# Where the lower halves of an attention output wait for their sum: a head pair's own denominator buffer, or the next pair's place in the output tile

## The chip, the cores and the metric

The kernel runs on one core of a Trainium2 chip. Its time is the device time in microseconds (us) of one execution. The engines are TensorE (PE, with its weight loads listed as PEld), VectorE (DVE), ScalarE (ACT), GpSimd (POOL) and SyncE (SP, which here only issues DMA transfers). Each engine works through its own instructions in order and waits at the first one whose inputs or buffers are not ready.

## The reference

Causal attention with a multiplicative decay, for 8 batches x 8 heads, 576 positions, head size 64, followed by a feed-forward layer with a squared ReLU over the 4608 rows of 512:

```python
scores = q @ k.T / sqrt(64) + (cum[:, None] - cum[None, :])   # cum = cumsum(log(clip(f)))
scores = where(causal, -1e9, scores)
attn = exp(scores - max(scores)); attn = attn / (sum(attn) + 1e-9)
x = attn @ v                                                  # 64 heads -> (4608, 512)
out = relu(x @ w_in) ** 2 @ w_out                             # 512 -> 2048 -> 512
```

## The kernel before

The 64 heads run one after the other. A head has six units (`UNITS`): a block of up to 128 keys against a range of queries. One unit is one **slot**, so there are 384 slots, and a written schedule says for each slot what is traced in it: the score products of its unit (`score`), the products with v of the unit two slots back (`av_part`, `LAG = 2`), parts of `finish`, events of the heads to come, and a share of the feed-forward steps (`fill`, `mlp_half`). PE, ACT, DVE and POOL execute in the order of tracing. SP's transfers are ordered by the tile framework.

The feed-forward layer works in 18 chunks of 256 rows; a chunk has 16 steps of two halves, `mlp1` (12 products of 256 columns) and `mlp2` (6 products of 512 columns). A batch has 576 rows, 2.25 chunks, so the 48 slots of a batch get the halves of two chunks of the batch before (4 halves to 3 slots), in one batch of three (2 halves to a slot). `ready[b]` says from which slot on batch b's rows are to be used, two slots after `finish` part 3 of its last pair. What is left after the last slot is feed-forward work alone.

From head 14 on (`NWHOLE`), values are split into a rounded upper half and a rest, and the product of v with the probabilities has two halves in one PSUM bank: rows 0 to 63 and rows 64 to 127. There is one such bank (`banks["av"] = [0]` once the feed-forward layer runs). When the query range 256 to 575 of a head is complete (first slot of the next head), ACT copies the two halves out of the bank: the first (line 502) into the head's place in `xts`, the output tile of the batch (two buffers, `xt0` and `xt1`, in turns, a place of 576 columns for each pair of heads), the second (line 504) into `xl`. Only then may PE write queries 0 to 255 of the head into the bank (line 464, one slot later); these are copied out in the same way.

`finish` runs once for each pair of heads, in four parts, at `(h + 1) * 6 - 1` plus the four numbers of `DIVIDE`, h being the odd head:

- part 0 loads the partial sums of the probabilities that `store_sums` (line 454) wrote to DRAM (line 526)
- part 1: DVE adds `xl` to x (line 535), reduces the sums and takes the reciprocals (537, 540), and two DMAs store them to DRAM (542)
- part 2 loads them again, spread over the partitions, into a tile named `den` (549)
- part 3: POOL multiplies x by `den` (551)

`xl` and part 2's tile share the name `den`, which has one buffer. Thus the `xl` of a pair can only be written when the multiplication of the pair before has read its reciprocals. With `(2, 4, 5, 6)`, and counting slots from the first slot of the even head that follows the pair, the parts lie in slots 1, 3, 4 and 5, and the next pair's first `xl` copy in slot 6.

Around it, in the slots of each head: POOL's selects of the causal mask (401), POOL's subtractions for the next head's lower halves (311 in slot 1, 314 in slot 3), DVE's rounding of q and k (303, 304 in slot 0), the row maxima of the next head (336 on PE, 342 on DVE; slots 1.5 to 4), which SP stores into the row that the next head's first score product reads (347), the cumulative row of the head after (257), and the split of finished x for the feed-forward layer (`split_x`, 568 and 569), which at the end of a batch is traced in the slot of part 3.

Of the kernel before, what the change touches and what calls it, by code (L numbers as in the profile page):

```python
# [9 lines left out]
F32 = mybir.dt.float32  # L10
# [26 lines left out]
def decay_attention_relu2_kernel(  # L37
# [20 lines left out]
    NH, D, _, S = qk.shape  # L58
    P = 2 * D
    H = 8  # L60
# [4 lines left out]
    NCC = DM // P  # L65
# [10 lines left out]
    NWHOLE = 14  # L76
    DEPTH = 4
    cpool = ctx.enter_context(tc.tile_pool(name="cpool", bufs=1))
    wk = ctx.enter_context(tc.tile_pool(name="wk", bufs=2))
# [5 lines left out]
    def bank(use):  # L85

        turn = banks[use] or banks["s"]
        b = turn.pop(0)
        turn.append(b)
        return psum.tile([P, 512], F32, name=f"bank{b}")  # L90
# [153 lines left out]
    NU = len(UNITS)  # L244
    state = {}
    xts = {}
# [27 lines left out]
    def replicated(h):  # L274

        return h // 2 == H // 2 - 1
# [179 lines left out]
    def av_split(st, acc, u, o, i, first, last):  # L456

        j = UNITS[u][0]
        ph, pl = st["p"][u]
        vhl = st["vhl"][:, j]  # L460
        high = acc[:, o], vhl, ph[:, i]
        low = acc[:D, o], vhl[:, :D], pl[:, i]
        for k, args in enumerate((high, low) if first else (low, high)):
            nc.tensor.matmul(*args, start=first and k == 0, stop=last and k == 1)  # L464

    def av_part(h, u, low):

        j, q0, q1 = UNITS[u]
        s0, s1 = (q0, min(q1, QA)) if low else (max(q0, QA), q1)
        if s0 >= s1:  # L470
            return
        st = state[h]
        first = u == (NU - 1 if low else 0)
        last = u == NU - 2
        if first:
            st["av"] = bank("av")
        acc = st["av"]
        base = 0 if low else QA
        o, i = slice(s0 - base, s1 - base), slice(s0 - q0, s1 - q0)
        if h < NWHOLE:  # L480

            vr = st["vr"].rearrange("p j d -> p (j d)")
            d = st["vr"].shape[2]
            vr = vr[:, j * d:min(j * d + P, NJ * d)]
            nc.tensor.matmul(acc[:vr.shape[1], o], vr, st["p"][u][:, i], start=first, stop=last)
        else:
            av_split(st, acc, u, o, i, first, last)
        if last:
            n = QA if low else S - QA
            if not low:  # L490
                if h % H == 0:
                    xts[h // H] = wk.tile([P, NCC, S], F32, name=f"xt{h // H % 2}", bufs=1)
                if replicated(h):

                    st["den"] = state[h - 1]["den"] if h % 2 else wk.tile(
                        [P, 2 * DM], F32, name=f"w{2 * NF - 3}", bufs=1,
                    )[:, :S]
                if h >= NWHOLE:
                    st["xl"] = state[h - 1]["xl"] if h % 2 else wk.tile([P, S], F32, name="den", bufs=1)
            o = (h % 2) * D  # L500
            x = xts[h // H][o:o + D, (h % H) // 2, base:base + n]
            nc.scalar.copy(out=x, in_=acc[:D, :n])
            if h >= NWHOLE:
                nc.scalar.copy(out=st["xl"][o:o + D, base:base + n], in_=acc[D:, :n])  # L504
            elif replicated(h):
                nc.scalar.copy(out=st["den"][o:o + D, base:base + n], in_=acc[D:, :n])
            else:
                nc.scalar.copy(out=qkraw[D:D + 1, h % 2, base:base + n], in_=acc[D:D + 1, :n])
# [142 lines left out]
    NA = H * NU  # L651


    DIVIDE = (2, 6, 9, 13), (2, 4, 5, 6)
    DIRECT = {1: 3, 3: 4}
    MAXIMA = (-3, -2.5, -2, -1.5, -1, -0.5), (1.5, 2, 2.5, 3, 3.5, 4)
    SPLIT = 0, 1, 1, 3
# [9 lines left out]

    def fin(h, part):

        return (h + 1) * NU - 1 + (DIRECT if replicated(h) else DIVIDE[h >= H])[part]  # L670

    avs = {}
    for n, (h, u) in enumerate(slots):
# [2 lines left out]
    for h in range(1, NH, 2):  # L676
        for part in DIRECT if replicated(h) else range(4):
            fins.setdefault(fin(h, part), []).append((h, part))
    last_slot = max(fins)
    ready = [fin(b * H + H - 1, 3) + 2 for b in range(B)]  # L680

    def fill(n, part):
# [79 lines left out]
    for n in range(-2 * NU, last_slot + 1):  # L762
        if n == 0:
            opening = len(tc.nc.cur_bb.bb.instructions)
        live = 0 <= n < len(slots)
        split_last()
        if live:
            h, u = slots[n]
            score(h, u)
            if h >= NWHOLE:  # L770
                unsplit.append((h, u))
        for ha, ua in avs.get(n, ()):
            if ua < NU - 1:
                av_part(ha, ua, False)
            else:
                av_part(ha, ua, True)
                av_part(ha, ua - 1, True)
        for args in fins.get(n, ()):
            finish(*args)
        for do in events.get((n, 0), ()):  # L780
            do()
        wr = RATES[0 if n < -9 else 1 if n < -6 else 2 if n < -3 else 3 if n < 0 else 4 if n < ready[0] else 5]
        cv(wr / 2)
        fill(n, 0.5)
        for do in events.get((n, 1), ()):
            do()
        cv(wr / 2)
        fill(n, 1.0)
# [45 lines left out]
```

## Time and profile before

| | |
|---|---|
| median of 3 runs | 1341.64 us (1337.22 to 1342.75) |
| the profiled execution's own time | 1340.81 us |
| its span, first to last instruction | 1338.8 us |
| PE busy / DVE / ACT / POOL | 1197.0 / 798.7 / 780.3 / 411.7 us |
| mean granted PE clock | 0.964 of full speed |

The span is 2.0 us shorter than the execution's own time. Up to about 228 us the first 14 heads and the preparation of the weights run, from there to about 1180 us the 50 heads with split values, then feed-forward work alone. An engine's busy time is an average over these stages; the idle time that stands in brackets in a timeline, with what ended it, tells where an engine waited.

### The profile page before, as it was taken

The page shows a single profiled execution, that of the slowest core. Times are in us where ns is not written, and L with a number is a line of the kernel's source. Part 1 is how long each engine was busy: PE and PEld are TensorE (multiplying, and loading weights), DVE is VectorE, ACT ScalarE, POOL GpSimd, SP SyncE. Part 2 cuts the span into 40 slices and gives each one's busy share as a digit, 9 for nine tenths or more (in the row PEclk, how much of TensorE's full clock was granted, in tenths as well). Part 3 has the DMA queues.
Part 4 walks back from the last instruction along what each step waited for, and adds up shares of the span by engine and source line. Part 5 has one row for each costly group of instructions (what it writes and reads, how often), then busy time and mean ns, then how long its engine had stood idle before and what let it go on. Part 6 is the DMA issues. An engine that isn't in the chain of part 4 may idle for free. (4 is left out here: it accounts for less than half of the span.)

```text
span 1338.8 us, 22723 instructions
## 1 busy us (share of the span) xinstructions
PE 1197.0 (89%) x7302; PEld 1053.6 (79%) x7302; DVE 798.7 (60%) x2132; ACT 780.3 (58%) x2008; POOL 411.7 (31%) x668
## 2 busy tenths in 40 slices
PE   4877999898888888999999888889988898989998
PEld 3556878787777777889899777778887787879997
DVE  7657665676666666666666666666666666631211
ACT  3655666566655665666666556656666556643443
POOL 4545452333333333322322233333332333200000
PEclk9989999999998999999999999999999999999999
DMA  7877612111211112111121111112111211000000
GB/s 190 185 160 171 165 35 53 39 41 30 55 38 43 37 39 54 30 41 38 41 55 19 50 33 46 39 39 50 30 46 39 54 34 46 20 26 1 17 16 16
DMA packets 124073, 72.36 MB, mean 54 GB/s; under 512 B 106008, under 2 KB 106008, under 8 KB 123956
## 3 DMA queue, kind: packets, MB, share of 16 engines
q1 hardware_dynamic: 122836, 66.80, 20.8%
q0 software_dynamic: 1120, 4.13, 1.6%
q8 instruction: 58, 0.95, 0.3%
q14 instruction: 59, 0.48, 0.1%
HBM read 60.36 MB, written 10.34 MB: 53 GB/s over the span
## 5 line engine op out<-in xcount | busy, mean ns | idle before, releaser
L604 PE MATMUL bank<-w,gh 128*128 128x512 f32 x1152 | 418.9, 405 | 0.0
L581 PE MATMUL bank<-xh,w 128*128 128x256 f32 x2304 | 346.8, 294 | 8.8 <-DVE xh L568 4.1
L581 PEld LDWEIGHTS bank<-xh,w 128*128 128x128 f32 x2304 | 312.2, 196 | 16.8 <-issue 4.9
L604 PEld LDWEIGHTS bank<-w,gh 128*128 128x128 f32 x1152 | 224.9, 195 | 40.8 <-ACT gh L591 0.3
L592 DVE TENSOR_TENSOR gl<-g,gh 128x256 fp32r<-128x256 f32 x288 | 122.6, 426 | 207.3 <-ACT gh L591 206.6
L604 PE MATMUL bank<-w,gl 128*128 128x512 f32 x576 | 232.3, 403 | 3.1 <-DVE gl L592 3.0
L589 ACT ACTIVATE r<-bank 128x256 f32<-128x256 f32 x288 | 110.1, 382 | 159.8 <-PE bank L581 146.4
L401 POOL TENSOR_SCALAR_AFFINE_SELECT p<-p 128x128 f32<-128x128 f32 x200 | 65.5, 327 | 415.5 <-ACT p L399 307.3
L581 PE MATMUL bank<-xl,w 128*128 128x256 f32 x1152 | 192.4, 291 | 0.0
L415 DVE TENSOR_TENSOR pl<-p,ph 128x320 fp32r<-128x320 f32 x200 | 133.8, 669 | 75.9 <-ACT ph L414 75.5
L464 PE MATMUL bank<-ph,vhl 128*128 128x320 f32 (+4 forms) x350 | 109.2, 312 | 71.2 <-ACT den L504 70.8
L581 PEld LDWEIGHTS bank<-xl,w 128*128 128x128 f32 x1152 | 166.0, 200 | 0.0
L342 DVE CUSTOM_DVE_ANT_0 bank<-bank,mz 128x256 f32<-128x256 f32 (+4 forms) x320 | 133.9, 433 | 22.3 <-PE bank L336 17.8
L464 PEld LDWEIGHTS bank<-ph,vhl 128*128 128x128 f32 x350 | 67.8, 194 | 86.4 <-ACT den L504 82.3
L415 DVE TENSOR_TENSOR pl<-wmag,ph 128x320 fp32r<-128x320 f32 x100 | 45.9, 459 | 146.3 <-ACT ph L414 146.3
L414 ACT CAST ph<-p 128x320 fp32r<-128x320 f32 x200 | 81.2, 406 | 87.8 <-POOL p L401 87.2
L336 PE MATMUL bank<-rk 66*128 66x320 f32 (+9 forms) x384 | 111.0, 318 | 18.9 <-DMA rk<-qkraw 10.7
L590 ACT ACTIVATE g<-r 128x256 f32<-128x256 f32 x288 | 120.5, 418 | 11.6 <-DVE gl L592 2.5
L604 PEld LDWEIGHTS bank<-w,gl 128*128 128x128 f32 x576 | 112.6, 195 | 17.7 <-DVE gl L592 4.0
L591 ACT ACTIVATE gh<-r 128x256 fp32r<-128x256 f32 x288 | 115.7, 402 | 0.0
L381 PE MATMUL bank<-rk 67*128 67x320 f32 (+4 forms) x300 | 90.0, 300 | 13.6 <-DMA rk<-tcol 12.3
L399 ACT ACTIVATE p<-bank 128x320 f32<-128x320 f32 x200 | 75.5, 378 | 37.5 <-PE bank L384 36.2
(94 smaller groups left out, 1791.2 us busy)
## 6 DMA issues: line engine op xcount, KB each, us to landing
qkraw<-in_qk SPq DMA_DIRECT2D x50, 288.0 KB
out<-osb SPq DMA_DIRECT2D x36, 256.0 KB
v<-in_v SPq DMA_DIRECT2D x56, 160.0 KB
den<-rdr SPq DMA_DIRECT2D x62, 144.0 KB
w<-in_w_in SPq DMA_DIRECT2D x16, 512.0 KB
w<-in_w_out SPq DMA_DIRECT2D x16, 512.0 KB
rk<-in_qk POOLq DMA_DIRECT2D x14, 288.0 KB, 5.3
rl<-in_qk SPq DMA_DIRECT2D x14, 288.0 KB
```

The source lines that it names most:

```text
L336: nc.tensor.matmul(ps[:m, :n], st["r2"][:rows, q0:q0 + m], st["kl0"][:rows, k0:k0 + n], start=True, stop=True,)
L342: nc.vector.tensor_tensor_reduce(out=ps[:m, :n], in0=ps[:m, :n], in1=mz[:m, mo:mo + n], op0=ALU.add, op1=ALU.min, scale=-1.0, scalar=init, ...
L381: nc.tensor.matmul(ps[:kn, :n], st["kl0"][:D + 3, k0:k0 + kn], st["r2"][:D + 3, q0:q1], start=True, stop=False,)
L414: nc.scalar.copy(out=ph[:, :n], in_=p[:, :n])
L415: nc.vector.tensor_tensor(out=pl[:, :n], in0=p[:, :n], in1=ph[:, :n].bitcast(F32), op=ALU.subtract,)
L464: nc.tensor.matmul(*args, start=first and k == 0, stop=last and k == 1)
L581: nc.tensor.matmul(ph[:, :T], w[:, s, cc], x[:, cc, :], start=(cc == 0 and k == 0), stop=(cc == NCC - 1 and k == 2),)
L589: nc.scalar.activation(out=r, in_=ph[:, :T], func=AF.Relu)
L590: nc.scalar.activation(out=g, in_=r, func=AF.Square)
L591: nc.scalar.activation(out=gh, in_=r, func=AF.Square)
L592: nc.vector.tensor_tensor(out=gl, in0=g, in1=gh.bitcast(F32), op=ALU.subtract)
L604: nc.tensor.matmul(po, g[:, ts], w[:, s], start=(fc == 0 and k == 0), stop=(fc == NF - 1 and k == 2),)
```

## The change

For heads 14 and up, `xl` no longer is a tile `den`. It is the next pair's place in the output tile (`pair = h // 2 + 1`; for the last pair of a batch that is the first place of the next batch's tile, which is therefore allocated one pair earlier; for the last pair of all a further tile). The parts of `finish` get a third row of `DIVIDE` for these heads, and the second row (now only heads 8 to 13) changes too:

```diff
-                if h % H == 0:
-                    xts[h // H] = wk.tile([P, NCC, S], F32, name=f"xt{h // H % 2}", bufs=1)
+                pair = h // 2 + 1
+                for b in (h // H, pair // NCC if h >= NWHOLE else 0):
+                    if b not in xts:
+                        xts[b] = wk.tile([P, NCC, S], F32, name=f"xt{b % 2}", bufs=1)
...
                 if h >= NWHOLE:
-                    st["xl"] = state[h - 1]["xl"] if h % 2 else wk.tile([P, S], F32, name="den", bufs=1)
+                    st["xl"] = xts[pair // NCC][:, pair % NCC, :]
...
-    DIVIDE = (2, 6, 9, 13), (2, 4, 5, 6)
+    DIVIDE = (2, 6, 9, 13), (2, 4, 6, 7), (3, 5, 6, 8)
...
-        return (h + 1) * NU - 1 + (DIRECT if replicated(h) else DIVIDE[h >= H])[part]
+        return (h + 1) * NU - 1 + (DIRECT if replicated(h) else DIVIDE[(h >= H) + (h >= NWHOLE)])[part]
```

Counted as above, the parts lie in slots 2, 4, 5 and 7 for heads 14 and up. `ready[b]` moves two slots with part 3 for batches 1 to 7.

## Rows read from the trace of the kernel before

**Rows 1.** the page: busy us of each engine over the whole span

```profile
PE 1197.0 (89%) x7302; PEld 1053.6 (79%) x7302; DVE 798.7 (60%) x2132; ACT 780.3 (58%) x2008; POOL 411.7 (31%) x668
```

**Rows 2.** PE's waits from 230 to 1180 us: total us, times, longest

```profile
PE bank L464 <- ACT den L504: 69.7, 40, 3.9
PE bank L381 <- DMA rk<-tcol: 12.3, 25, 0.9
```

**Rows 3.** waits of all engines over the span: total us, times, longest

```profile
POOL xt L551 <- DMA den<-rdr: 99.2, 31, 17.3
...
ACT den L504 <- POOL xt L551: 54.5, 24, 3.7
...
DVE xh L568 <- POOL xt L551: 40.1, 7, 6.7
```

**Rows 4.** PE's timeline: start us, us, what, in brackets the wait before it

```profile
266.80 0.58 PE L464 MATMUL bank<-ph,vhl 128*128 128x256 f32 x1 [3.43 <-ACT den L504]
...
1106.60 0.31 PE L381 MATMUL bank<-rk 67*128 67x320 f32 x1
...
1111.04 0.25 PE L381 MATMUL bank<-rk 67*128 67x192 f32 x1
...
1121.48 0.39 PE L381 MATMUL bank<-rk 67*128 67x320 f32 x1 [0.47 <-DMA rk<-tcol]
...
1123.54 0.31 PE L381 MATMUL bank<-rk 67*128 67x320 f32 x1
...
1127.06 0.58 PE L464 MATMUL bank<-ph,vhl 128*128 128x256 f32 x1 [3.05 <-ACT den L504]
...
1132.04 0.25 PE L381 MATMUL bank<-rk 67*128 67x192 f32 x1
...
1163.05 0.38 PE L464 MATMUL bank<-ph,vhl 128*128 128x256 f32 x1 [1.75 <-ACT den L504]
```

**Rows 5.** POOL's timeline around the same two heads

```profile
1109.20 0.29 POOL L401 TENSOR_SCALAR_AFFINE_SELECT p<-p 128x128 f32<-128x128 f32 x1 [4.39 <-ACT p L399]
1109.46 1.42 POOL L311 TENSOR_TENSOR rl<-qkraw,rk 64x576 fp32r<-64x576 f32 x1
1112.47 0.29 POOL L401 TENSOR_SCALAR_AFFINE_SELECT p<-p 128x128 f32<-128x128 f32 x1 [1.59 <-DVE tcol L342]
...
1125.16 1.40 POOL L551 TENSOR_TENSOR xt<-xt,den 128x576 f32<-128x576 f32 x1 [3.41 <-DMA den<-rdr]
```

**Rows 6.** stretches: length, busy us of engines, granted PE clock, DMA share, GB/s

```profile
1127.06:1145.55 18.49, 17.47 (x104) 15.86 (x104) 13.26 (x34) 12.17 (x33) 5.74 (x9) 0.91 0.17 49
...
655.00:740.00 85.00, 85.00 (x565) 77.94 (x564) 53.36 (x143) 56.51 (x146) 24.41 (x39) 1.00 0.16 38
...
266.00:573.00 307.00, 270.51 (x1665) 242.96 (x1665) 199.74 (x551) 187.96 (x491) 100.96 (x153) 0.94 0.17 41
...
763.00:1180.00 417.00, 370.21 (x2302) 332.52 (x2302) 270.67 (x743) 257.16 (x674) 136.10 (x208) 0.95 0.17 39
```

**Rows 7.** SP's timeline: transfers issued around the long wait

```profile
1117.78 1.15 SPq L542 DMA_DIRECT2D rdr<-sums  x2
1119.03 1.79 SPq L347 DMA_DIRECT2D rk<-tcol  x3
1121.24 1.14 SPq L549 DMA_DIRECT2D den<-rdr  x2
1122.48 0.39 SPq L257 DMA_DIRECT2D rk<-cum_dr  x1
```

**Rows 8.** timeline of POOL and DVE in the batch with three chunks

```profile
613.21 1.43 POOL L551 TENSOR_TENSOR xt<-xt,den 128x576 f32<-128x576 f32 x1 [0.85 <-DMA den<-rdr]
613.29 1.50 DVE L428 TENSOR_TENSOR wmag<-wmag,p 128x128 f32<-128x128 f32 x1
```

**Rows 9.** DVE's timeline: the last read of an output tile's part

```profile
1135.59 0.96 DVE L569 TENSOR_TENSOR xl<-xt,xh 128x768 fp32r<-128x768 f32 x1
```

**Rows 10.** PE's timeline where the attention has ended

```profile
1195.51 2.04 PE L581 MATMUL bank<-xh,w 128*128 128x256 f32 x8 [4.14 <-DVE xh L568]
```

## The prediction

> **What bounds the kernel now.** I read the page first. PE is busy for 1197.0 us of 1338.8 [rows 1], no other engine for more than 60% of it, so PE sets the time and what matters is where PE stands still or runs slowly. PE's own waits in the 50 split heads come next: one line holds nearly everything, 69.7 us in 40 waits of line 464 for ACT's copy out of the single accumulator bank [rows 2]. A second line, 12.3 us in 25, waits for the row maxima. The list of all waits then shows what stood behind that copy: ACT's `xl` copy waited 54.5 us in 24 cases for POOL's multiplication, and that one waited for the transfer of the reciprocals, 99.2 us in 31 [rows 3]. So the chain is: reciprocals land, POOL multiplies, `den` comes free, ACT copies `xl`, PE may write the bank.
>
> PE's timeline splits the 40 waits. Twenty are long, from 3.43 us (the first, at 266.80) to 1.75 us (the last, at 1163.05) [rows 4]; added up they are 59.1 us, 2.95 each. They belong to the even heads, whose `xl` is the first into `den`. The other twenty are 69.7 - 59.1 = 10.6 us, 0.53 each: the odd heads, whose `xl` goes into a tile already free, and who wait just for the two copies. The batch with three chunks (about 573 to 763 us) has none: with two halves in every slot its slots are long enough, and PE is busy for 85.00 of 85.00 us [rows 6].
>
> The waits cost twice. In 655 to 740 us the granted clock is 1.00; in the head that begins with the wait at 1127.06 it is 0.91 over 18.49 us [rows 6]: after such a wait PE has stretches at the lower level, 1.2 instead of 2.4 GHz. Over the two-chunk stretches it is 0.94 (307 us) and 0.95 (417 us).
>
> **The change part by part.**
>
> *The long waits.* The next pair's place is written by nobody before slot 6 of the following head pair and was last used a batch earlier, so the even head's copies find it free, like the odd head's now. 20 x (2.95 - 0.53) = 48.4 us go. Bounds: nothing gained if another condition holds the copy (below), 59.1 if even the ordinary wait is covered. I take 48.4.
>
> *The clock.* Lost time is 0.06 x 307 + 0.05 x 417 = 39 us [rows 6]; by the one head, 0.09 x 18.49 = 1.7 us each, it is 20 x 1.7 = 33. Heads with only the short wait return to the full level, so I expect the loss to go with the long waits, and take 36. Bounds: 0 (the clock falls anyway) and 39. A check by the slots: with the long wait it is 8.50 us from the score product at 1123.54 to that at 1132.04, without it 4.44 (1106.60 to 1111.04) [rows 4]. The difference, 4.06, is 2.5 of wait and 1.5 of clock, and 20 x 4.06 = 81, against my 48.4 + 36 = 84.4, in which the batch ends weigh more.
>
> *SP's order.* Part 1 moves from slot 3 to slot 4, and its two reciprocal stores with it. SP issues the stores at 1117.78 for 1.15 us, and only then three transfers of row maxima, 1.79 us [rows 7]. The first of these three (slot 3) is the one that the next head's score product needs; it came 0.47 us late at 1121.48 [rows 4]. Two of the three should now go ahead of the stores. Of the 12.3 us most belong to heads with these stores: bounds 0 and 12.3, I take 8 gained.
>
> *When the reciprocals land now.* The stores move back by two transfers (2/3 of 1.79, 1.2 us), and so do the loads: `den` was there at 1125.16 [rows 5], now about 1126.3. Slot 7 begins at 1123.54 less the 0.47, at 1123.1. In a head without a long wait POOL's select of that slot starts 2.6 us after the score product (1106.60 to 1109.20) and takes 0.29 [rows 4, 5], so POOL reaches the multiplication at 1126.0 and waits 0.3 us instead of 3.41. Behind it are the 1.40 us of the multiplication, then 1.42 of the subtraction in line 311, to 1129.1; the next select is due 5.9 us after the score product (1106.60 to 1112.47), at 1129.0. That just fits. What has no cover left is small: if `den` lands later, selects, ACT's and DVE's roundings and, two slots on, PE's products with v are late by as much.
>
> *DVE beside POOL.* Today the multiplication falls into the stall. In slot 7 DVE is at work. In the three-chunk batch, where POOL multiplies at 613.21 for 1.43 us, a DVE addition of 128 columns that starts at 613.29 ends only with it, after 1.50 us [rows 8]. So DVE can lose between 0 and 1.4 us for each pair. Whether PE feels it: bounds 0 and 24 x 1.4 = 34 us. There PE had no wait, but its slots are long. I take 0.2 us each, 5 us. The Trainium skill ("SBUF — State Buffer", section "Who interferes with whom") says that a DVE instruction with two SBUF inputs and a GpSimd one that reads SBUF share a read interface, and that the later one stands until the other is done. The trace agrees with its 1.50 us. By that rule alone each pair pays a whole multiplication and the sum below would be 1254.4 - 5 + 34 = 1283; by my value it is 1254.4. It speaks against this change, and is a rival below.
>
> *The cumulative row.* SP issues it right behind the loads of `den` (1122.48) [rows 7]; they come about 1.2 us later now, while the maxima that read the row lose the cover of the long wait. Bounds 0 to 0.5 us in each pair; I take 3 us in all.
>
> *Ends of batches.* `split_x` stays in the slot of part 3, so DVE still waits there for POOL (40.1 us in 7 [rows 3]). With `den` landing about when it is asked for, 5.7 us become some 2. PE's share in this is already in the long waits; I count nothing more. The output tile's earlier allocation needs the buffer's last reader gone: the read that began at 1135.59 ended at 1136.55 [rows 9], and the copies that would now write there are those before PE's resumption at 1163.05 [rows 4], 26 us later; two slots take some 5 us of that. No cost.
>
> *The tail.* After the last slot PE waits 4.14 us for the last split [rows 10]. Part 1 comes one slot later, and the feed-forward halves are stretched by two slots, so the chain is longer by one slot of pure feed-forward work and covered by two: at 4/3 halves to a slot of some 1.4 us each, 1.9 us gained. I take 2.
>
> *Heads 8 to 13* get one slot more before part 2: POOL's wait there delays little on PE. Nothing counted, 2 us either way.
>
> The sum, against the profiled execution's 1340.8 us: 1340.8 - 48.4 - 36 - 8 - 2 + 5 + 3 = **1254.4 us**. The median of the runs shown is 0.8 us above that execution, so 1255.
>
> **The rivals.**
>
> *A new wait in slots 7 to 9.* POOL's multiplication and line 311 back to back hold DVE's operands or the selects, and PE stands for about 1 us in each of 24 pairs: 24 us more than the sum, 1278, or 1288 where some of these also cost clock. For it: the 1.50 us addition [rows 8] and a fit with no reserve on POOL. Against: PE's products use results two slots old, and a slot with two halves gives 4.4 us. The rule of the "SBUF" page in the Trainium skill is this rival's mechanism. Chance 0.11.
>
> *The clock falls all the same.* The waits go, but the two short waits in slots 6 and 7 are enough to lower it once for each pair: 1254 + 36 = 1290. Against: the odd heads have the short wait too, and keep the clock. Chance 0.06.
>
> *The change doesn't do what it says.* ACT's copy waits for something else of the output tile, an earlier reader of the buffer or the addition of part 1, which reads the place that the next pair's x is copied to. Then about 1340. Against: the addition is traced two slots ahead of that copy, and the buffer is free 26 us ahead. Chance 0.04.
>
> *Slower.* One mechanism: the reciprocals land so late that POOL, standing at the multiplication in slot 7, holds the selects behind it and with them PE. In the old place POOL's wait cost 4.1 us for a pair. POOL would be through with line 311 at 1129.1, and PE can bear about 2 us more; so it decides when `den` lands some 6 us later than I work out, and at 7 us all 24 pairs pay 1 us more than before: 1365. Nothing on SP's queue between stores and loads takes so long. Chance 0.03.
>
> **How the numbers follow.** My forecast has 0.76. The time is its own, 1255. Its own spread: all gains and no cost, with 39 for the clock and 12 for the row maxima, is 1340.8 - 48.4 - 39 - 12 - 2 = 1239; with DVE's and the row's costs at half their bounds, about 1268. The range goes up to the first rival's 1288 and leaves out the last three: 1240 to 1288. Under 0.5% (6.7 us) a change of this kernel can't be told from none. Faster by more: 0.76 + 0.11 + 0.06 = 0.93; within: 0.04; slower: 0.03.
>
> **What would show it.** Right: no wait of ACT for POOL's multiplication, PE's waits at the v products all about 0.5 us, 25 to 30 us in all; granted clock 0.99 or 1.00 between 266 and 1100 us; two-chunk batches shorter by about 16 us and the three-chunk one nearly unchanged; two row-maxima transfers ahead of the reciprocal stores on SP. Wrong: POOL still waits over 2 us for `den`; DVE's rounding in slots 7 and 8 above 1.5 us with PE waiting for it; a clock below 0.97 without long waits.

## The result and the profile after

The changed kernel takes 1234.4 us (median of 4 runs, 1231.83 to 1238.2), the kernel before, run beside it, 1339.4 us (4 runs, 1336.16 to 1342.75). The ratio is 0.9218, with a 95% interval from 0.918 to 0.9256: faster by 105 us where 86 were forecast, and 5.6 us below the lower end of the range. The profiled execution took 1231.83 us, with a span of 1230.0. The lines of the kernel after stand 4 lower from about line 492 on: 502 is now 506, 504 is 508, 542 is 546, 549 is 553, 551 is 555, 568 is 572, 581 is 585, 589 is 593, 592 is 596, 604 is 608.

The page of the changed kernel: busy us of each engine, as in [rows 1].

```profile
PE 1158.4 (94%) x7302; PEld 1020.7 (83%) x7302; DVE 820.5 (67%) x2132; ACT 787.3 (64%) x2008; POOL 409.3 (33%) x668
```

PE has the same 7302 instructions and is busy for 38.6 us less: the same products at a mean granted clock of 0.994 instead of 0.964. DVE has the same 2132 instructions and is busy for 21.8 us *more*; to that we come back.

PE's waits in the split heads of the changed kernel: total us, times, longest, as in [rows 2].

```profile
PE bank L336 <- DVE rk L304: 17.2, 38, 0.8
PE bank L381 <- DVE tcol L342: 5.3, 5, 3.2
PE bank L464 <- ACT xt L508: 1.8, 2, 1.2
...
PE bank L381 <- DMA rk<-tcol: 1.0, 2, 0.5
```

The waits for ACT's copy out of the bank were 69.7 us in 40. The twenty long ones are gone, as forecast; but the twenty short ones, which were to stay, are gone too, but for 1.8 us in 2. The row maxima's transfers are late for 1.0 us instead of 12.3. Two waits are new, and the forecast's sum has neither: 17.2 us in 38 (1.5 in 2 before), at the products for the row maxima (line 336), for DVE's rounding of q and k; and 5.3 us in 5, at the score products (line 381), for DVE's row maxima (line 342). The five stand in heads 17, 25, 33, 49 and 57, right behind the ends of batches.

Waits of POOL and DVE over the whole span after, as in [rows 3].

```profile
POOL xt L555 <- DMA den<-rdr: 27.6, 7, 17.2
...
DVE xh L572 <- POOL xt L555: 14.1, 7, 3.4
```

The wait in the middle of [rows 3], ACT's for POOL's multiplication, has no counterpart any more. POOL's waits for the reciprocals fall from 99.2 us in 31 to 27.6 in 7; one of some 17 us, at the last multiplication of all, is in both.

Three stretches of the changed kernel (two chunks, three chunks, two chunks), columns as in [rows 6].

```profile
266.00:527.00 261.00, 252.83 (x1657) 229.51 (x1656) 202.90 (x542) 189.16 (x486) 101.33 (x150) 0.99 0.21 48
527.00:700.00 173.00, 171.19 (x1123) 155.42 (x1122) 117.33 (x297) 114.52 (x296) 49.32 (x79) 1.00 0.16 40
700.00:1054.00 354.00, 340.99 (x2237) 307.62 (x2236) 280.40 (x740) 253.56 (x654) 136.01 (x203) 1.00 0.20 47
```

The granted clock is 0.99 to 1.00 where it was 0.94 and 0.95.

Where the 109 us between the two spans went follows from three marks on PE's timeline, head 14's first score product, head 63's first, and the end:

| stretch | before | after | difference |
|---|---|---|---|
| up to head 14 | 208.5 | 204.4 | -4.1 |
| heads 14 to 62 | 950.4 | 850.0 | -100.4 |
| rest | 180.0 | 175.5 | -4.5 |

In the middle stretch PE is busy for 859.65 us before and 821.36 after (clock 0.96 and 1.00), and idle for 90.8 and 28.7. The 38.3 us of busy time are not clock alone: of the feed-forward products of 256 columns the stretch holds 24 fewer after, the two halves that now come behind the start of head 63. At 1.10 us for eight (line 585 at 307.86, shown below) they are some 3 us. So about 35 us of the 100 are clock, 3 are work that moved, and 62 are waits.

### The profile page after: what moved, and what is told of

Read it like the earlier page. It is cut to its first block, busy times and chain, and to the rows that moved or that the text cites. A ratio compares the mean times of both kernels' runs of the same rounds, so it can differ in the third digit from the quotient of the medians.

```text
span 1230.0 us, 22744 instructions
## 1 busy us (share of the span) xinstructions
PE 1158.4 (94%) x7302; PEld 1020.7 (83%) x7302; DVE 820.5 (67%) x2132; ACT 787.3 (64%) x2008; POOL 409.3 (33%) x668
## 4 chain that ended last, share of the span: by engine, by line
PE 42%; DVE 6%; ACT 5%; issue 2%; DMA 1%; POOL 0%; SPq 0%; POOLq 0%; DVEq 0%; ACTq 0%
PE bank L585 18%; PE bank L608 17%; PE bank L464 3%; PE bank L336 2%; PE bank L384 1%; PE bank L381 1%; DVE wmag L428 1%; ACT ph L414 1%; DVE pl L415 1%; DVE bank L342 1%; DMA den<-rdr 1%; DVE gl L596 1%; ACT g L594 1%; ACT xt L508 1%; ACT r L593 1%
## 5 line engine op out<-in xcount | busy, mean ns | idle before, releaser
L585 PE MATMUL bank<-xh,w 128*128 128x256 f32 x2304 | 330.3, 286 | 4.2 <-DVE tcol L342 2.2
L585 PEld LDWEIGHTS bank<-xh,w 128*128 128x128 f32 x2304 | 302.3, 190 | 11.5 <-DVE tcol L342 2.3
L608 PEld LDWEIGHTS bank<-w,gh 128*128 128x128 f32 x1152 | 217.6, 189 | 38.8 <-ACT gh L595 0.3
L585 PE MATMUL bank<-xl,w 128*128 128x256 f32 x1152 | 185.2, 283 | 0.0
L415 DVE TENSOR_TENSOR pl<-p,ph 128x320 fp32r<-128x320 f32 x200 | 119.4, 597 | 63.4 <-ACT ph L414 60.4
L585 PEld LDWEIGHTS bank<-xl,w 128*128 128x128 f32 x1152 | 158.4, 190 | 0.0
L336 PE MATMUL bank<-rk 66*128 66x320 f32 (+9 forms) x384 | 118.7, 324 | 34.8 <-DVE rk L304 17.2
L428 DVE TENSOR_TENSOR wmag<-wmag,p 128x320 f32<-128x320 f32 (+3 forms) x250 | 127.2, 509 | 1.7
L336 PEld LDWEIGHTS bank<-rk 66*128 66x128 f32 (+3 forms) x384 | 70.0, 185 | 48.3 <-DVE rk L304 22.6
L464 PE MATMUL bank<-ph,vhl 128*128 128x320 f32 (+4 forms) x350 | 103.1, 295 | 2.4 <-ACT xt L508 2.4
```

The costliest lines, as they stand in the source:

```text
L336: nc.tensor.matmul(ps[:m, :n], st["r2"][:rows, q0:q0 + m], st["kl0"][:rows, k0:k0 + n], start=True, stop=True,)
L415: nc.vector.tensor_tensor(out=pl[:, :n], in0=p[:, :n], in1=ph[:, :n].bitcast(F32), op=ALU.subtract,)
L428: nc.vector.tensor_tensor(out=total[:, q0:q1], in0=total[:, q0:q1], in1=p, op=ALU.add,)
L585: nc.tensor.matmul(ph[:, :T], w[:, s, cc], x[:, cc, :], start=(cc == 0 and k == 0), stop=(cc == NCC - 1 and k == 2),)
L608: nc.tensor.matmul(po, g[:, ts], w[:, s], start=(fc == 0 and k == 0), stop=(fc == NF - 1 and k == 2),)
```

## The experiments

Two things stood against each other as causes. The change moves `xl` to another buffer, and it moves the parts of `finish`; with part 3, though, `ready[b]` moves by two slots, and the feed-forward halves are paced from `ready[b]`. At 4 halves to 3 slots the slots of a head that get two halves are numbers 1 and 4 before, and 0 and 3 after (counted from 0 within a head). I call this the *phase* of the halves. The phase can be set by itself with a constant in `fill`:

```diff
-        r0 = ready[b - 1]
-        r1 = ready[b] if b < B else r0 + H * NU
+        r0 = ready[b - 1] + PACE * (b > 1)
+        r1 = ready[b] + PACE if b < B else r0 + H * NU
```

**The buffer alone (e1_buffer_only).** The changed kernel with the old slots:

```diff
-    DIVIDE = (2, 6, 9, 13), (2, 4, 6, 7), (3, 5, 6, 8)
+    DIVIDE = (2, 6, 9, 13), (2, 4, 5, 6), (2, 4, 5, 6)
```

> The kernel before with xl in the next pair's place and nothing else; all numbers of DIVIDE as before, so the feed-forward halves stand in the same slots. Phase theory (the part of the gain that I missed comes from the two slots by which ready moves: the slot in which ACT copies the bank then holds two halves instead of one, and hides the copies): the long waits go, the short ones of about 0.5 us stay in all 40 heads, the row maxima still come late; 1250 to 1262 us, some 20 us of PE waiting for the copies. Slots theory (the later parts themselves brought it, by SP's order and POOL's freedom): also 1250 to 1262. If the buffer is worth all of it: 1233.

Measured: 1295.2 us, ratio 0.9679 (0.9637 to 0.972). That is 33 us above the upper end of what I expected: the later parts are worth far more than I took. PE's largest waits from 226 to 1150 us:

```profile
PE bank L464 <- ACT xt L508: 17.2, 34, 1.0
PE bank L464 <- DVE pl L415: 17.2, 5, 4.7
PE bank L381 <- DMA rk<-tcol: 14.4, 25, 1.3
```

The first line is the step of the forecast by itself: the copies' long waits are gone, the short ones stay, 0.5 us each. The second is new, and with it most of what is lost lies at the ends of the batches: against the same kernel with the later parts and the same slots for the feed-forward halves (e2 below), heads 14 to 62 take 23.5 us longer, and 19 of these fall on the five pairs of heads behind such an end. PE, POOL and DVE there, each from its own timeline of this kernel:

```profile
553.82 0.58 PE L464 MATMUL bank<-pl,vhl 128*64 128x256 f32 x2 [2.81 <-DVE pl L415]
...
554.41 2.02 PE L585 MATMUL bank<-xh,w 128*128 128x256 f32 x8
```

```profile
551.18 1.40 POOL L555 TENSOR_TENSOR xt<-xt,den 128x576 f32<-128x576 f32 x1 [3.15 <-DMA den<-rdr]
```

```profile
552.61 0.36 DVE L572 CAST xh<-xt 128x256 fp32r<-128x256 f32 x1 [5.78 <-POOL xt L555]
```

Read them from POOL on: `split_x` is queued on DVE in the slot of part 3 and stands 5.78 us for POOL, which stands for the reciprocals. Behind it on DVE is the remainder `pl` (line 415, at 553.35) that PE's v product needs; PE waits 2.81 us, and the eight products of line 585 that follow take 2.02 us (granted clock 0.50, the lower level, from 553.80 to 557.00) instead of the 1.10 that they take at the full level (at 307.86 below). In the kernel before, DVE stood there as long, but most of it lay inside PE's long wait for the bank, and little was seen as PE's own, from 230 to 1180 us:

```profile
PE bank L464 <- DVE pl L415: 3.5, 5, 1.0
```

DVE's waits at this place are 39.6 us in 7, as before the change; with the later parts they are 14.1.

**The phase, four ways.** The changed kernel with the phase of before (PACE = 1) and with the third one there is (PACE = 2), the kernel before with the phase of after (PACE = 2), and the buffer alone with the phase of after (the first experiment with PACE = 2):

> The changed kernel with the pacing of the halves one slot later still, three slots after the kernel before, which puts the two-halves slots where they were (4 halves to 3 slots repeat every 3 slots). Phase theory: the short waits come back in 40 heads, 1245 to 1260 us, the row maxima stay in time. Slots theory: no change, 1230 to 1238, since parts and buffer are those of the changed kernel.

> The kernel before with the pacing alone two slots later; xl still in den. Phase theory: a second half of 1.4 us stands in front of each wait for the copies, so the short waits vanish and the long ones shrink from 2.95 to about 1.5 us, some without a fall of the clock: 1270 to 1310. A rival by which the pacing does it all and the buffer nothing: 1235. Slots theory: 1335 to 1342.

> The first of these kernels (xl moved, DIVIDE as before) with the pacing two slots later, as ready sets it in the changed kernel. Phase theory: buffer and pacing are the whole change, 1230 to 1240. Slots theory: like the first, 1250 to 1262, with row maxima still late by about 0.5 us in half of the heads.

> The changed kernel with the pacing two slots later still: the third of the three places that the slots with two halves can have (slots 2 and 5 of a head). Phase theory: the slot of the copies has one half again and so has the next one, the short waits return in 40 heads with 0.5 to 1 us: 1250 to 1275. If only the number of slots mattered and not where the halves stand: 1230 to 1238.

Median us, with the interval of the ratio to the kernel before that ran beside each (1334.8 us for the first four of these kernels, 1341.4 for the third phase):

| | old phase | new phase | third phase |
|---|---|---|---|
| old buffer, old slots | 1339 (before) | 1319.8 (0.9823 to 0.9912) | |
| new buffer, old slots | 1295.2 (0.9637 to 0.972) | 1272.0 (0.9484 to 0.9548) | |
| new buffer, new slots | 1269.9 (0.9466 to 0.9531) | 1234.4 (0.918 to 0.9256) | 1316.2 (0.9767 to 0.9848) |

All directions were expected and most sizes missed: the old phase costs 35 us where I had expected 11 to 26, the third one 82 where I had expected 16 to 41, and the two kernels with the new phase and old slots stay above their ranges by 10 and 32. By the ratios, times 1339.4 us and good to some 5 us, all three parts have a share that none of the others replaces: the buffer 43 and 47 us, the slots 24 and 40, the phase 18, 22 and 37, each more where the others are there already. The old buffer with the new slots was not run.

Why the phase matters is seen where PE asks for the bank. PE's timeline of the changed kernel with the old phase, from the slot in which ACT copies:

```profile
481.86 0.31 PE L381 MATMUL bank<-rk 67*128 67x320 f32 x1
...
482.45 0.40 PE L608 MATMUL bank<-w,gh 128*128 128x512 f32 x1
...
483.85 0.31 PE L381 MATMUL bank<-rk 67*128 67x320 f32 x1
...
485.06 0.39 PE L464 MATMUL bank<-ph,vhl 128*128 128x256 f32 x1 [0.76 <-ACT xt L508]
```

ACT's timeline of the same kernel:

```profile
484.16 0.42 ACT L506 COPY xt<-bank 64x320 f32<-64x320 f32 x1
484.59 0.42 ACT L508 COPY xt<-bank 64x320 f32<-64x320 f32 x1
```

And the changed kernel itself, PE, then ACT:

```profile
307.26 0.31 PE L381 MATMUL bank<-rk 67*128 67x320 f32 x1
...
307.86 1.10 PE L585 MATMUL bank<-xh,w 128*128 128x256 f32 x8
...
309.28 0.40 PE L608 MATMUL bank<-w,gh 128*128 128x512 f32 x1
...
310.67 0.31 PE L381 MATMUL bank<-rk 67*128 67x320 f32 x1
...
310.97 0.28 PE L464 MATMUL bank<-ph,vhl 128*128 128x256 f32 x1
...
311.97 0.39 PE L336 MATMUL bank<-rk 66*128 66x256 f32 x1 [0.42 <-DVE rk L304]
```

```profile
308.22 0.42 ACT L506 COPY xt<-bank 64x320 f32<-64x320 f32 x1
308.65 0.42 ACT L508 COPY xt<-bank 64x320 f32<-64x320 f32 x1
```

In the old phase the slot of the copies holds one half and lasts 1.99 us (481.86 to 483.85); the second copy ends at 485.01, and PE stands from 484.30. In the new phase it holds two halves and lasts 3.41 us; the second copy ends at 309.07, and PE asks at 310.97. So in every head of the two-chunk batches PE has feed-forward work in just the time in which the only bank is emptied. The total of that wait with the old phase, and the largest waits with the third:

```profile
PE bank L464 <- ACT xt L508: 38.4, 38, 1.4
```

```profile
PE bank L585 <- ACT r L593: 35.3, 35, 1.5
PE bank L464 <- POOL p L401: 29.3, 32, 0.9
```

The Trainium skill ("Perfetto Trace Analysis", section "Optimization Strategy") reads a gap that repeats on the busiest engine as a possible lack of buffers. Here a second bank would be that cure, which was not run; the 38 waits fell to 2 with the bank as single as before, by the order of the work alone.

With the old slots the same shift gives less (18 and 22 us), and other waits take the place: in the kernel before with the new phase 46.9 us in 38 for the rounding of q and k and still 24.4 in 22 for `den`, and with the buffer alone and the new phase (e4) 35.5 us for the rounding and 12.0 at the ends of batches. The kernel before with the new phase, PE's waits:

```profile
PE bank L336 <- DVE rk L304: 46.9, 38, 2.0
PE bank L464 <- ACT den L504: 24.4, 22, 3.7
```

**The new wait (e6_round_half_earlier).** DVE takes the rounding of q and k behind the subtraction of a feed-forward result (line 596), which in the new phase has become ready just then. DVE's timeline of the changed kernel ahead of the 0.42 us wait at 311.97:

```profile
310.76 0.42 DVE L596 TENSOR_TENSOR gl<-g,gh 128x256 fp32r<-128x256 f32 x1 [0.68 <-ACT gh L595]
311.10 0.45 DVE L303 CAST rk<-qkraw 64x576 fp32r<-64x576 f32 x1
311.47 0.45 DVE L304 CAST rk<-qkraw 64x576 fp32r<-64x576 f32 x1
```

DVE is idle for 0.68 us and then does three things in a row. The edit takes part 0 of the preparation, which holds these two roundings, half a slot earlier; parts 1 to 3 stay:

```diff
-                at((h - 1) * NU + SPLIT[part], 1, prep, h, part)
+                at((h - 1) * NU + SPLIT[part], int(part > 0), prep, h, part)
```

> The changed kernel with DVE's and ACT's rounding of q and k (part 0 of the preparation) half a slot earlier, ahead of the slot's first feed-forward half. The 17.2 us in 38 cases that PE waits at the row maxima's products for line 304 should go if they come from the rounding standing behind a feed-forward subtraction in DVE's order: 1215 to 1225. Rival: the rounding then holds DVE and ACT ahead of that half and the wait moves to the feed-forward products: 1230 to 1245.

Measured: 1223.0 us, ratio 0.9113 (0.9069 to 0.9156), as expected. No wait at line 336 for line 304 is left; the stretch of heads 14 to 62 shrinks from 850.0 to 839.6 us.

**The second row of shares (e7_second_row_old).**

```diff
-    DIVIDE = (2, 6, 9, 13), (2, 4, 6, 7), (3, 5, 6, 8)
+    DIVIDE = (2, 6, 9, 13), (2, 4, 5, 6), (3, 5, 6, 8)
```

> The changed kernel with the second row of DIVIDE (heads 8 to 13) as before, (2, 4, 5, 6). The stretch before head 14 was 4.1 us shorter after the change, which I had counted at nothing. If the second row did that: 1236 to 1240, with head 14's first score product near 208 instead of 204 us. If it is the pacing of the first two chunks over two slots more, or chance: 1232 to 1236.

Measured: 1240.4 us, ratio 0.924 (0.9202 to 0.9278). By time it can't be told from the changed kernel. In the trace it can: from head 9's first score product to head 14's it is 93.5 us here, and 89.3 to 89.4 in the changed kernel and in all four that keep its second row and its phase. By this pair the row is worth 4.2 us. The other kernels put it between 2.4 and 5.3: with the old row the kernel before, e1, e3 and e4 take 91.8, 93.7, 92.2 and 92.2, with the new row and other phases e2 and e5 take 88.4 and 88.7. Ahead of head 9 the times scatter more, from 112.4 to 119.4 us in five kernels that do the same up to there (the changed one, e6, e8, e10 and e11).

**SP's order (e8_sums_early).** The third row with the stores of the reciprocals one slot earlier, where they stood before:

```diff
-    DIVIDE = (2, 6, 9, 13), (2, 4, 6, 7), (3, 5, 6, 8)
+    DIVIDE = (2, 6, 9, 13), (2, 4, 6, 7), (2, 4, 5, 8)
```

> The changed kernel with parts 0 to 2 in their old slots for heads 14 and up and part 3 where it is now, (2, 4, 5, 8): the reciprocal stores go ahead of the three row maxima again. My step on SP's order (8 us gained because two row maxima pass the stores): row maxima late by about 0.5 us in half of the heads, 1238 to 1246. Rival: with two halves in slot 5's neighbourhood the row maxima have time anyway: 1230 to 1238. The reciprocals land earlier than now, so nothing should be lost at the ends of batches.

Measured: 1227.1 us, ratio 0.9144 (0.9097 to 0.919): my expectation, slower than the changed kernel, falls. That it is faster is not clear by time, the two intervals overlap; heads 14 to 62 take 846.9 us for 850.0. SP's timelines, first the changed kernel, then this one:

```profile
318.91 1.59 SPq L347 DMA_DIRECT2D rk<-tcol  x2
321.15 1.14 SPq L546 DMA_DIRECT2D rdr<-sums  x2
322.39 0.52 SPq L347 DMA_DIRECT2D rk<-tcol  x1
```

```profile
322.01 1.46 SPq L546 DMA_DIRECT2D rdr<-sums  x2
323.58 2.30 SPq L347 DMA_DIRECT2D rk<-tcol  x3
325.98 1.18 SPq L553 DMA_DIRECT2D den<-rdr  x2
```

The order changed just as the prediction said, two maxima ahead of the stores, and here it is changed back, with all three behind, as in [rows 7]. And the wait for the maxima is 0.3 us in all. With the phase of after, then, SP's order doesn't matter to PE. With the old phase it may: the wait is 14.4 us in 25 with the old slots (e1) and names no transfer at all with the new ones (e2); the order alone was not changed there.

**Both gains together (e10_both), and one more step (e11_split_later).** The first has the edits of the sixth and the eighth experiment. (Its expectation speaks of every rounding part but the first, and of transposes at line 336; the edit moves part 0 alone, and line 336 holds products of q and k.) The second adds:

```diff
-        at(ready[b] - 1 - (b > 0), 0, split_x, b * S // T, b + 1)
+        at(ready[b] - 1 - (b == B - 1), 0, split_x, b * S // T, b + 1)
```

> The changed kernel with two edits together that were each run alone: every rounding part but the first half a slot earlier (alone 1223.0 us beside the changed kernel's 1234), and the third row of shares back at four slots, (2, 4, 5, 8) (alone 1227.1). If they take away different waits, the gains of 11 and 7 us add: 1212 to 1220 us, with PE's waits in front of the row maxima's transpose both for VectorE and for the transfer below 2 us in all. Rival: both shorten the same waits (TensorE's 17.2 us at the transposes of line 336 for VectorE, which the rounding half a slot earlier took away alone): then 1221 to 1225 us, no better than the better one.

> The kernel of the run before with the split of the next batch's x put one slot later in its queue, for all batches but the last. In the changed kernel VectorE stands 14.1 us in 7 places at that split, waiting for POOL, and pairs at the ends of batches take 34 to 37 us instead of 32.3. If this stand is what lengthens them, the split one slot later finds POOL's work done: VectorE's wait falls below 4 us, the pairs at the ends of batches take 33 to 34 us, and the time is 6 to 15 us below that of the run before: 1202 to 1212 us. Rival: the pairs are longer for the batch's own work (its first half comes with the split, and TensorE waits for that instead): then within 4 us of the run before, or above it.

Measured: 1219.2 us, ratio 0.9091 (0.9046 to 0.9136), and 1216.8 us, ratio 0.9069 (0.9017 to 0.9122). The first lies within what was expected of adding gains, but its interval overlaps that of the sixth experiment; the stretch of heads 14 to 62 tells it better: 850.0 after, 839.6 and 846.9 with one edit, 835.4 with both, so 10.4 and 3.1 us shorter alone, and 14.6 together. At line 336 no wait is left; at the score products that need the row maxima they come to 9.8 us (6.6 for VectorE's maxima, 3.2 for the transfer), not below 2. For the second the rival was right, it is within 4 us. PE's largest waits in heads 14 to 62, first kernel, then second:

```profile
PE bank L381 <- DVE tcol L342: 6.6, 5, 3.2
PE bank L381 <- DMA rk<-tcol: 3.2, 6, 0.7
PE bank L381 <- DVE gl L596: 2.5, 5, 0.6
```

```profile
PE bank L381 <- DVE gl L596: 3.4, 6, 0.7
PE bank L585 <- DVE xh L572: 3.4, 5, 0.9
PE bank L381 <- DMA rk<-tcol: 2.6, 4, 0.8
PE bank L585 <- DVE xl L573: 2.5, 4, 0.9
```

DVE's stand for POOL at the split falls from 11.9 us to 1.5, but the split then comes late for the first half that uses it, and PE waits 5.9 us there, while at line 342's maxima it waits 5.0 less. Both versions beat both kernels.

## Why the prediction was right or wrong

*Right: the chain and the clock.* The wait of ACT for POOL's multiplication is gone and with it all twenty long waits. With the buffer alone the wait for the copies falls from 69.7 us in 40 to 17.2 in 34, by 52.5 where 48.4 were forecast. The clock's 36 us are 36 by the granted clock of heads 14 to 62, 0.960 before and 0.998 after (0.040 x 950.4 - 0.002 x 850.0).

*Wrong: the sum's first term, 20 x (2.95 - 0.53) = 48.4.* It measured 66.3 us (in heads 14 to 62, from 68.7 to 2.4). The step that failed is "the even head's copies find it free, like the odd head's now": it holds the odd head's wait of 0.53 us fixed. That wait depends on how much work PE has between its last write into the bank and the next, and the change moved it. The prediction had the move in hand, in "the feed-forward halves are stretched by two slots", and drew from it only the number of halves, for the tail; in which slots of a head they come to stand, it did not ask. With the phase of before the changed kernel takes 1270 us.

*That also means that 1255 was too low for what it described.* With the phase held, as the sum assumed, the short waits do not stay at 10.6 us but grow to 38.4 in 38, 1.0 each. The buffer alone, in the same phase but with the old slots, leaves them at 0.5 us each (17.2 in 34), so the growth comes with the later parts; by what way, I haven't separated. The good phase (35 us), which was luck, hid an error of 15 in the other direction.

*The row maxima: size about right, cause not needed.* 8 forecast, 11.3 measured. SP's order came as described, and with the old phase the new slots do end that wait (e1 against e2), though 8.1 us of waits for VectorE's maxima stand there instead. With the new phase the wait is gone in either order (0.3 us in e8). So this gain would have come without the step that was to bring it, and the step adds nothing to it here. Of the 11.3 us, 5.3 come back at the same products as waits for VectorE's maxima, from another cause (under *DVE beside POOL*).

*Ends of batches: "I count nothing more".* About right in the sum, but only because part 3 moved as well: the buffer alone leaves 17.2 us of PE's waits there, 34 us of stretches at the lower clock, and 1295 us in all, and with part 3 alone moved among these heads (e8) no such wait is left. The step missed that the long wait for the bank covered DVE's stand. Each stand is 2.0 us now (14.1 in 7), as forecast.

*DVE beside POOL: the mechanism is there, with another partner, and PE feels little of it.* I took 5 us between 0 and 34, for POOL's multiplication. Groups of DVE's instructions of the changed kernel from 226 to 1060 us, busy us and mean ns:

```profile
L428 DVE TENSOR_TENSOR wmag<-wmag,p 128x320 f32<-128x320 f32 (+3 forms) x240 | 123.5, 515 | 1.6
...
L572 DVE CAST xh<-xt 128x1024 fp32r<-128x1024 f32 (+3 forms) x18 | 16.9, 941 | 10.7 <-POOL xt L555 10.7
```

In the kernel before, from 230 to 1180 us, these were 379 and 557 ns. Over the same heads, 14 to 62, the 244 additions take 93.7 us before and 125.1 after, the 18 casts 10.0 and 16.9: 38 us more. Line 415 takes 15 us less (176.7 and 161.7), so DVE's net is 23 us in these heads and 21.8 over the span. One addition, and POOL beside it:

```profile
329.75 1.68 POOL L311 TENSOR_TENSOR rl<-qkraw,rk 64x576 fp32r<-64x576 f32 x1
```

```profile
330.07 1.72 DVE L428 TENSOR_TENSOR wmag<-wmag,p 128x320 f32<-128x320 f32 x1
```

Alone such an addition takes 0.48 us. The rule that the prediction weighed, from the Trainium skill ("SBUF — State Buffer", section "Who interferes with whom"), is that a VectorE instruction with two SBUF inputs contends with a GpSimd one that reads SBUF. The pair agrees with it: 1.72 us. By that rule alone, each pair paying on PE, the time would have been 1283.

But POOL's partner here is not the multiplication that the prediction priced. Of the 38 slow additions of line 428 in heads 14 to 62, one lies beside it (line 555), 16 beside the subtraction of line 311, which stands right behind it on POOL (the multiplication runs from 328.37 for 1.43 us, line 311 starts at 329.75), 19 beside line 322 and two beside line 314. The 19 come with the new phase: in the old one (e2) there are none.

None of PE's waits names line 428. The casts are another matter. At the ends of batches the cast of the split meets line 311, as here, where it takes 1.64 us; in the kernel before, the same cast took 0.43 us (at 419.64):

```profile
394.41 1.64 DVE L572 CAST xh<-xt 128x512 fp32r<-128x512 f32 x1 [1.75 <-POOL xt L555]
```

The row maxima stand behind it on DVE, and PE's next score product waits 0.54 us for them at 397.35. The 5.3 us in 5 are the five places of this kind. So the rival of a new wait in slots 7 to 9 came, but for 5 us and not 24; that the slow cast brings it, with DVE's stand of 1.75 us ahead of it, is read from the timeline and was not tested by itself. The larger new wait (17.2 us at line 336) isn't from the lock but from the phase, as the kernel before with the new phase (46.9 us) and the sixth experiment show.

*The cumulative row: 3 us forecast, none measured.* No wait of PE in the changed kernel names its transfer (line 257).

*Heads 8 to 13: "nothing counted".* From head 9 to head 14 it is 91.8 us before and 89.3 after, 2.5 gained. The row is worth 4.2 by its own experiment, and 2.4 to 5.3 over all kernels.

*The tail: 2 us forecast, 4.5 measured.* PE's wait of 4.14 us [rows 10] is now 1.26:

```profile
1088.29 1.19 PE L585 MATMUL bank<-xh,w 128*128 128x256 f32 x8 [1.26 <-DVE xh L572]
```

The cover by "two slots" does not explain it: with the later parts and the old or third phase, which stretch the halves by three and four slots, the rest takes 179.6 and 179.4 us, and with the old slots and the new phase 176.1. So it goes with the phase too. By what way is open: the work left for this stretch differs as well (1052 products of PE before, 1082 after, 1088 and 1100 in the two others).

The sum of these differences against the profiled execution: 16.0 us more in heads 14 to 62 (100.4 for 84.4), 4.1 ahead of them (2.5 from head 9 on, the rest within the scatter of the start), and 2.5 more in the tail, make 22.6, from 1254.4 to 1231.8. The 16.0 are themselves a balance. Against the forecast's terms the copies gave 17.9 us more, the row maxima's transfers 3.3, the cumulative row 3, smaller waits 5.1 and PE's busy time 2.3; the wait at line 336 took 15.7 of this back. DVE's 5 us came out as 5.3, by luck: from line 311 and at the ends of batches, not from the multiplication in each pair. So the term that failed most is the first, and the new wait hid most of its error.

## What to carry to other kernels

When a change moves an event from which other work is paced, write down which slot that work will stand in afterwards, not only how much of it there is: here the same 4 halves in 3 slots gave 1234, 1270 and 1316 us. A short wait that is the same in every head is no constant of the machine; ask what the engine could be doing meanwhile, and try each phase, which is one number to change. A long wait covers others: before its removal is counted, look at what else was late during it and where that will stand next.

## What the runs showed of the hardware

Beside one of POOL's subtractions, DVE's additions of 320 columns took 1.72 us (line 311) or 1.12 us (line 322) instead of 0.48, and a cast of 512 columns 1.64 us instead of 0.43. Two groups of DVE's instructions need 38 us more by it, all of DVE 21.8 us more; of this at most 5.3 us appear as waits of PE, whose clock was at 0.99 to 1.00.

The clock's loss did not follow the number of waits, nor the idle time in all. 38 waits of about 0.5 us (17.2 us in all) leave it at 0.99 to 1.00, and twenty of 2.95 us had it at 0.94 and 0.95. In heads 14 to 62 PE is idle for 90.8 us in the kernel before, with waits of up to 3.9 us, at a clock of 0.96, and for 93.8 us with the third phase, with waits of up to 2.3 us, at 0.99. Single waits show it too: one of 2.81 us is followed by products at half the speed, 2.02 us for 1.10 (e1), and in the changed kernel one of 3.16 us, at 265.37, by a granted clock of 0.50 from 266.20 to 269.60.
